# Attention and SwiGLU in one kernel: two-bank exps in the first batch, a ring of single PSUM banks, and x transposed by DMA from batch 2 on

## Chip, cores, metric

One core of one Trainium2 chip. The metric is the device time of one execution in microseconds; executions of one kernel here lie up to 1.4% apart (413.16 to 418.88 us for the kernel before). The profile is one such execution; its span is some 2 us shorter than the time.

## The reference

```python
# q, k, v: (8 batches, 8 heads, 576, 64), s: (8, 8, 576); x: (4608, 512)
cum    = np.cumsum(np.maximum(s, 0.0), axis=-1)
scores = q @ k.T / 8 + np.minimum(-(cum[..., :, None] - cum[..., None, :]), 0)   # causal
attn   = softmax(scores) @ v
x      = attn.transpose(0, 2, 1, 3).reshape(4608, 512)
out    = (silu(x @ w_gate) * (x @ w_val)) @ w_out                                # d_ff = 1536
```

## The kernel before

Per head, scores are computed transposed (keys on partitions), exponentiated, multiplied by V ("AV" below) and normalised into `ot`, tokens on partitions. The FFN needs x with features on partitions, so each pair of heads is transposed. Nine FFN tiles of 512 tokens are woven with the attention of the next batch: after every FFN step of four matmuls, `pump` emits the attention pieces that are due. The program fixes the order of emission for each engine and for the DMA queue of the sync engine (SP); in the traces of before, after, e3 and e4 no SP instruction that issues a DMA starts before the one ahead of it has ended. PSUM, the memory into which TensorE writes its results, is divided by these kernels into eight banks of 512 fp32 columns.

```python
# PSUM: three pools
scp = tile_pool("scp", bufs=3, PSUM); avp = tile_pool("avp", bufs=1, PSUM)
mp  = tile_pool("mp", bufs=4, PSUM)
...
def x_pe(pr):                                   # x of one pair of heads
    ...
    ps = mp.tile([128, S], BF16, tag="m", name="xps")
    for c in range(NCH):                        # 5 chunks of tokens: 4 x 128, 64
        n = 128 if c < 4 else TAIL
        nc.tensor.transpose(ps[:, c*128 : c*128+n], ot[0:n, c, :], ident[0:n, 0:n])
    n0 = TT - 64 * b
    nc.vector.tensor_copy(xts[b + 1][:, r, 0 : S - n0], ps[:, n0:S])
    nc.vector.tensor_copy(xts[b][:, r, TT - n0 : TT], ps[:, 0:n0])
...
# K/Q of head blocks 2 to 4 (a block is four heads), directly ahead of their scores
if not first and step == 0 and 2 <= h < NPE:
    ...
    cast_one(h, "k", nc.gpsimd); cast_one(h, "q", nc.gpsimd)
    ...
    for g in range(2):
        for nm in ("k", "q"):
            pe_transpose(h, nm, g)
            pe_out(h, nm, g, 0, nc.vector); pe_out(h, nm, g, 1, nc.scalar)
...
LAG = 1.65       # heads by which the FFN runs behind the attention
```

From block 5 on, K and Q are cast on GpSimd, stored to DRAM, and brought back by two large DMA transposes per block (`pk<-ks`, `pq<-qs`), on SP like all loads and stores except the weights.

The softmax here doesn't subtract the row's maximum and nothing guards it: scores larger than these inputs give would overflow.

## Time and profile before

| | before |
|---|---|
| time, median of the runs at the start | 414.88 us |
| span of the profiled run | 411.9 us |
| first FFN matmul | 36.3 us |
| one steady period (an FFN tile with eight heads) | 42.1 us |
| TensorE / VectorE / ScalarE / GpSimd busy | 93 / 61 / 51 / 30% |

Busy shares average over stages with different limits. I read periods from the first output copy (`ysb`) of one tile to that of the next. How SP waited in the kernel before is in its own list of waits (who waited for whom: us in total, times, longest); a queue that waits 141 us for results has that much room:

```profile
SPq L490 <- ACT ysb L489: 140.8, 28, 31.1
SPq L198 <- POOL cq L194: 40.8, 11, 4.5
SPq L198 <- POOL ck L194: 31.1, 6, 9.8
```

### The profile page before, as it was taken

How to read it: one execution, taken by the hardware profiler on the slowest of the kernel's cores; microseconds unless marked ns; L12 is line 12 of the kernel's file. 1: busy time of each engine (PE TensorE's matmuls, PEld its weight loads, DVE VectorE, ACT ScalarE, POOL GpSimd, SP SyncE). 2: the span in 40 equal slices, each digit the busy share in tenths (PEclk: the TensorE clock that was granted, in tenths of full speed). 3: DMA queues.
4: the chain of work that ended last, by engine and by line, in shares of the span. 5: the costliest groups of instructions: out<-in, count | busy, mean ns of one | idle time of the engine just before them, and what ended most of it. 6: DMA issues, size and time to landing. Idle time of an engine off the chain costs nothing.

```text
span 411.9 us, 7992 instructions
## 1 busy us (share of the span) xinstructions
PE 383.5 (93%) x3082; PEld 211.9 (51%) x3082; DVE 251.0 (61%) x494; ACT 212.0 (51%) x421; POOL 125.2 (30%) x224
## 2 busy tenths in 40 slices
PE   2687797989999999999999999999999999999996
PEld 1464454645555555555555555555555544444442
DVE  7846666366873588358844884479446733752750
ACT  7463665666555555456545564565556532322321
POOL 4783252743262316131623162316211110000000
PEclk9989998999999999999999999999999999999999
DMA  7999998466845793469346924681410002002002
GB/s 265 146 230 221 268 245 266 122 193 164 210 109 173 179 228 94 148 199 245 81 132 207 260 81 108 216 175 51 116 57 2 2 27 76 0 10 95 0 4 100
DMA packets 85335, 56.71 MB, mean 138 GB/s; under 512 B 65552, under 2 KB 69584, under 8 KB 85296
## 3 DMA queue, kind: packets, MB, share of 16 engines
q1 hardware_dynamic: 81360, 51.40, 44.8%
q0 software_dynamic: 3936, 4.79, 6.9%
q8 instruction: 24, 0.39, 0.4%
q14 instruction: 15, 0.12, 0.1%
HBM read 37.90 MB, written 15.93 MB: 131 GB/s over the span
## 4 chain that ended last, share of the span: by engine, by line
PE 90%; DVE 4%; DMA 2%; ACT 1%; POOL 1%; issue 1%; ACTq 0%; POOLq 0%
PE pg L457 23%; PE py L481 23%; PE pv L470 22%; PE sc L269 11%; PE av L305 7%; PE xps L337 3%; DVE kq L240 2%; DMA kq<-HL 1%; ACT pt L277 1%; DMA s_sb<-in_s_dram 1%; POOL vt L136 1%; PE tps L225 1%; DVE ot L321 1%; DVE c L167 0%; PE avm L305 0%
## 5 line engine op out<-in xcount | busy, mean ns | idle before, releaser
L277 ACT ACTIVATE pt<-sc 128x512 bf16<-128x512 f32 (+1 forms) x256 | 117.7, 505 | 56.2 <-PE sc L269 54.8
L464 DVE SCALAR_TENSOR_TENSOR pp<-th,pg 128x512 bf16<-128x512 bf16 x108 | 74.1, 686 | 63.8 <-ACT th L462 63.4
L457 PE MATMUL pg<-xt,wg 128*128 128x512 bf16 x432 | 111.8, 381 | 0.0
L470 PE MATMUL pv<-xt,wv 128*128 128x512 bf16 x432 | 110.9, 379 | 0.0
L462 ACT ACTIVATE th<-pg 128x512 bf16<-128x512 f32 x108 | 64.5, 597 | 86.0 <-PE pg L457 86.0
L481 PE MATMUL py<-wo,ht 128*128 128x512 bf16 x432 | 105.7, 379 | 0.0
L269 PE MATMUL sc<-kq 128*128 128x128 bf16 (+4 forms) x576 | 76.4, 247 | 10.4 <-DVE kq L240 5.5
L281 POOL TENSOR_SCALAR_AFFINE_SELECT pt<-pt 128x512 bf16<-128x512 bf16 x64 | 40.8, 637 | 140.0 <-ACT pt L277 137.7
L475 DVE TENSOR_TENSOR ht<-pp,pv 128x512 bf16<-128x512 bf16 x108 | 73.9, 684 | 7.9
L269 PEld LDWEIGHTS <-kq 128*128 128x128 bf16 x576 | 46.9, 101 | 44.3 <-issue 7.0
L457 PEld LDWEIGHTS <-wg 128*128 128x128 bf16 x432 | 38.5, 98 | 36.3 <-issue 0.8
L470 PEld LDWEIGHTS <-wv 128*128 128x128 bf16 x432 | 38.4, 98 | 34.8
L481 PEld LDWEIGHTS <-ht 128*128 128x128 bf16 x432 | 38.2, 98 | 34.9
L305 PEld LDWEIGHTS <-pt 128*128 128x128 bf16 x960 | 41.2, 98 | 20.9 <-issue 3.0
L305 PE MATMUL av<-vt,pt 128*128 128x65 bf16 x900 | 47.4, 194 | 2.0 <-POOL vt L136 0.9
L489 ACT ACTIVATE ysb<-py 128x512 f32<-128x512 f32 x36 | 21.5, 598 | 43.6 <-PE py L481 42.4
L286 POOL TENSOR_SCALAR_AFFINE_SELECT pt<-pt 128x64 bf16<-128x64 bf16 x64 | 15.4, 240 | 64.5 <-ACT pt L277 64.4
L341 DVE COPY xt<-xps 128x64 bf16<-128x64 bf16 (+7 forms) x32 | 9.7, 304 | 34.7 <-PE xps L337 34.7
L321 DVE TENSOR_TENSOR ot<-av,rc 128x320 bf16<-128x320 f32 x60 | 29.5, 491 | 2.1
L320 DVE RECIPROCAL rc<-av 128x5 f32<-128x5 f32 x60 | 11.4, 189 | 31.3 <-PE av L305 31.2
L136 POOL CAST vt<-rawv 128x512 bf16<-128x512 f32 (+1 forms) x40 | 25.7, 673 | 0.0
L240 DVE COPY kq<-tps 64x640 bf16<-64x640 bf16 (+1 forms) x24 | 17.5, 762 | 2.3 <-PE tps L225 2.1
(47 smaller groups left out, 160.6 us busy)
## 6 DMA issues: line engine op xcount, KB each, us to landing
rawk<-in_k_dram SPq DMA_DIRECT2D x16, 576.0 KB
rawq<-in_q_dram SPq DMA_DIRECT2D x16, 576.0 KB
out_dram<-ysb SPq DMA_DIRECT2D x36, 256.0 KB
rawv<-in_v_dram SPq DMA_DIRECT2D x32, 256.0 KB
ks<-ck SPq DMA_DIRECT2D x11, 288.0 KB
qs<-cq SPq DMA_DIRECT2D x11, 288.0 KB
wg<-in_moe_w_gate_dram POOLq DMA_DIRECT2D x2, 768.0 KB, 8.8
wv<-in_moe_w_val_dram POOLq DMA_DIRECT2D x2, 768.0 KB, 10.1
```

The lines of the kernel that those rows point to most:

```text
L136: eng.tensor_copy(VT[b % 2][0:n, c, :, 0:D], loaded["v", b][0:n, c, :, :])
L269: nc.tensor.matmul(sc[:, o : o + w], T[:, 0, e * S + 128 * tj : e * S + 128 * (tj + 1)], T[:, 1, e * S + lo : e * S + hi], start=True, sto ...
L277: nc.scalar.activation(pt[:, CHUNK_PT[ci] : CHUNK_PT[ci] + o], sc[:, 0:o], AF.Exp, scale=0.125)
L281: nc.gpsimd.affine_select(pt[:, 1088:1600], pt[:, 1088:1600], pattern=[[0, 4], [1, 128]], compare_op=ALU.is_ge, fill=zreg, base=0, channel ...
L305: nc.tensor.matmul(av[:, bi * (D + 1) : (bi + 1) * (D + 1)], pt[:, c0 : c0 + 128], VT[b % 2][:, tj, h, :], start=(tj == 0), stop=(tj == bi),)
L321: nc.vector.tensor_mul(ot[:, :, e * D : (e + 1) * D], av3[:, :, 0:D], rc[:, :, None].to_broadcast([128, NCH, D]),)
L457: nc.tensor.matmul(pg, WG[j][:, c, f0 : f0 + 128], xt[:, c, :], start=(c == 0), stop=(c == 3),)
L462: nc.scalar.activation(th, pg, AF.Tanh, scale=0.5)
L464: nc.vector.scalar_tensor_tensor(pp, in0=th, scalar=1.0, in1=pg, op0=ALU.add, op1=ALU.mult)
L470: nc.tensor.matmul(pv, WV[j][:, c, f0 : f0 + 128], xt[:, c, :], start=(c == 0), stop=(c == 3),)
L475: nc.vector.tensor_mul(ht, pp, pv)
L481: nc.tensor.matmul(py, hts[ft][:, ts_ * 128 : (ts_ + 1) * 128], WO[ft // WKO][:, ft % WKO, :], start=(ft == 0), stop=(ft == NFT - 1),)
```

## The change

The intent is to take x's transposes off TensorE, to halve the number of exps of batch 0, to let any PSUM bank serve any use, and to prepare K and Q of blocks 2 to 4 a block ahead. The core of the diff (cuts marked by ...):

```diff
-    scp = ... ; avp = ... ; mp = ...                       # three PSUM pools
+        bank["w", 0..1] = psa.tile([128, 1024], FP32)      # batch 0: two wide, four single
+        bank["s", 0..3] = psa.tile([128, 512], FP32)
+        ... second_psum(): eight single banks, taken in order of release
...
+            if b >= 2:                                     # in x_pe
+                for c in range(NCH):
+                    lo, end = c * 128, min(S, c * 128 + 128)
+                    while lo < end:
+                        hi = min(end, n0) if lo < n0 else end
+                        dst = (xts[b][:, r, TT - n0 + lo : TT - n0 + hi] if lo < n0
+                               else xts[b + 1][:, r, lo - n0 : hi - n0])
+                        nc.sync.dma_start_transpose(dst, ot[lo - c*128 : hi - c*128, c, :])
+                        lo = hi
+                return
...
+                if ahead and step == 0:                    # K/Q one block ahead
+                    cast_one(h + 1, "k", nc.gpsimd); cast_one(h + 1, "q", nc.gpsimd)
+                        if ahead and ci == 1 and step: prep_one(h + 1, step - 1)
...
-        load_v(0, range(5))
+        load_v(0, range(3))        # chunks 3, 4 later; w_load("g", 0), ("v", 0) earlier;
+                                   # casts of V at head 2 instead of head 1
-        LAG = 1.65
+        LAG = 2.65
```

More of the change, by code (lines that the diff above doesn't have):

```diff
@@ L51 @@
     NWCH = DF // WCH
-    DIAG_OFF = [1088, 1216, 1344, 1472, 1024]
-    OFF_OFF = {0: 0, 3: 448, 1: 512, 2: 832}
+    DIAG_OFF = [1088, 1216, 1344, 1472, 512]
+    OFF_OFF = {0: 576, 3: 1024, 1: 0, 2: 320}
     PTW = 1600
@@ L61 @@
     ]
-    CHUNK_PT = [1088, 0, 512, 1024]
+    CHUNK_PT = [1088, 576, 0, 512]
     def pt_col(tj, bi):
@@ L77 @@
     yp = ctx.enter_context(tc.tile_pool(name="yp", bufs=3))
-    scp = ctx.enter_context(tc.tile_pool(name="scp", bufs=3, space=PSUM))
-    avp = ctx.enter_context(tc.tile_pool(name="avp", bufs=1, space=PSUM))
-    mp = ctx.enter_context(tc.tile_pool(name="mp", bufs=4, space=PSUM))
     dram = ctx.enter_context(
@@ L105, with take, give, second_psum @@
         loaded = {}
-        SRC = {"k": (k, 0), "q": (q, 1)}
+        SRC = {"q": (q, 0), "k": (k, 1)}
+        first_psum = ExitStack()
+        psa = first_psum.enter_context(tc.tile_pool(name="psa", bufs=1, space=PSUM))
+        bank = {}
+        for i in range(2):
+            bank["w", i] = psa.tile([128, 1024], FP32, name=f"wide{i}")
+        for i in range(4):
+            bank["s", i] = psa.tile([128, 512], FP32, name=f"one{i}")
+        released = {key: i - 8 for i, key in enumerate(bank)}
+        clock = [0]
+        OPEN = 1 << 40
+        def take(kind="s"):
+            b = min((x for x in bank if x[0] == kind), key=lambda x: released[x])
+            assert released[b] < OPEN
+            released[b] = OPEN
+            return b
+        def give(b):
+            clock[0] += 1
+            released[b] = clock[0]
+        def second_psum():
+            assert all(x < OPEN for x in released.values())
+            at_end = dict(released)
+            first_psum.close()
+            psb = ctx.enter_context(tc.tile_pool(name="psb", bufs=1, space=PSUM))
+            bank.clear()
+            released.clear()
+            for i in range(8):
+                bank["s", i] = psb.tile([128, 512], FP32, name=f"bank{i}")
+                released["s", i] = at_end["w", i // 2] if i < 4 else at_end["s", i - 4]
+        def view(b, w):
+            return bank[b][:, 0:w]
+        def view16(b, w):
+            return bank[b][:, 0 : w // 2].bitcast(BF16)
         def load_one(hb, name, rs=(0, NR)):
@@ L136, in cast_v @@
             eng.tensor_copy(VT[b % 2][0:n, c, :, 0:D], loaded["v", b][0:n, c, :, :])
-        nc.sync.dma_start(s_sb, s.rearrange("b h n -> (b h) n"))
-        load_qk(0)
-        load_qk(1)
-        load_v(0, range(5))
         ONES2 = 1.0019378662109375
@@ L148, in aug_rows @@
             return KQ[i][r][r0 : r0 + 64, :, :].bitcast(FP32)
-        nc.vector.memset(warm, 0.0)
-        nc.scalar.activation(warm, warm, AF.Exp)
-        nc.vector.memset(one_s, 1.0)
-        nc.vector.memset(HL[:, 2:4, 0, :].bitcast(FP32), NEGS2)
-        nc.vector.memset(HL[:, 0:2, 1, :].bitcast(FP32), ONES2)
-        make_identity(nc, ident)
-        for e in range(2):
-            nc.gpsimd.memset(aug_rows(0, e)[:, 1, :], ONES2)
-            nc.gpsimd.memset(aug_rows(0, e)[:, 0, :], 0.0)
-            nc.scalar.copy(
-                KQ[1][e][64 * (1 - e) : 64 * (1 - e) + 64, 1, :],
-                one_s[:, 0:1].to_broadcast([64, NR * S + 64]),
-            )
-        nc.vector.memset(aug_rows(1, 0)[:, 0, :], 0.0)
-        nc.vector.tensor_scalar(s_sb, s_sb, 0.0, 8.0, ALU.max, ALU.mult)
-        nc.vector.tensor_tensor_scan(c8, one_s, s_sb, 0.0, ALU.mult, ALU.add)
-        nc.vector.tensor_copy(HL[:, 0, 0, :], c8)
-        nc.vector.tensor_sub(HL[:, 1, 0, :], c8, HL[:, 0, 0, :])
-        nc.vector.tensor_copy(HL[:, 2:4, 1, :], HL[:, 0:2, 0, :])
-        for r in range(2):
-            for i in range(2):
-                nc.vector.memset(KQ[i][r][64 * r : 64 * r + 64, :, NR * S :], 0.0)
         def aug(hb, engs):
@@ L178, in aug @@
                 r0 = 64 * (1 - r)
+                bh = hb * HB + hh
                 engs[hh].dma_start(
                     KQ[hb % 2][r][r0 : r0 + 4, :, e * S : (e + 1) * S],
-                    HL[hb * HB + hh : hb * HB + hh + 1, :, :, :],
+                    HL[bh : bh + 1, :, :, :],
                 )
+        nc.sync.dma_start(s_sb, s.rearrange("b h n -> (b h) n"))
+        load_qk(0)
+        load_qk(1)
+        load_v(0, range(3))
+        nc.vector.memset(warm, 0.0)
+        nc.scalar.activation(warm, warm, AF.Exp)
+        nc.vector.memset(one_s, 1.0)
+        nc.vector.memset(HL[:, 0:2, 0, :].bitcast(FP32), ONES2)
+        nc.vector.memset(HL[:, 2:4, 1, :].bitcast(FP32), NEGS2)
+        make_identity(nc, ident)
+        for r in range(2):
+            nc.gpsimd.memset(aug_rows(0, r), 0.0)
+            nc.scalar.mul(
+                KQ[1][r][64 * (1 - r) : 64 * (1 - r) + 64, 0, :],
+                one_s[:, 0:1].to_broadcast([64, NR * S + 64]), 0.0,
+            )
+        for r in range(2):
+            nc.gpsimd.memset(aug_rows(1, r)[:, 1, :], 0.0)
+            for i in range(2):
+                nc.gpsimd.memset(KQ[i][r][64 * r : 64 * r + 64, :, NR * S :], 0.0)
+        nc.vector.tensor_scalar(s_sb, s_sb, 0.0, 8.0, ALU.max, ALU.mult)
+        nc.vector.tensor_tensor_scan(c8, one_s, s_sb, 0.0, ALU.mult, ALU.add)
+        nc.vector.tensor_copy(HL[:, 0, 1, :], c8)
+        nc.vector.tensor_sub(HL[:, 1, 1, :], c8, HL[:, 0, 1, :])
+        nc.vector.tensor_copy(HL[:, 2:4, 0, :], HL[:, 0:2, 1, :])
         SP4 = [nc.sync] * 4
@@ L221, in pe_transpose @@
             j0, j1 = JG[g]
-            ps = mp.tile([128, j1 - j0, 128], BF16, tag="m", name="tps")
+            bs = take()
+            ps = view16(bs, (j1 - j0) * 128).rearrange("p (j x) -> p j x", x=128)
             ct = cts[name, hb]
@@ L227, in pe_transpose @@
                 )
-            tps[name, g] = ps
+            tps[name, g] = [ps, bs, 2]
         def pe_out(hb, name, g, r, eng):
@@ L235, in pe_out @@
             )[:, :, j0:j1]
-            srcp = tps[name, g][64 * r : 64 * r + 64].rearrange("a j x -> a x j")
+            tp = tps[name, g]
+            srcp = tp[0][64 * r : 64 * r + 64].rearrange("a j x -> a x j")
             if eng is nc.scalar:
@@ L240, in pe_out @@
                 eng.tensor_copy(dst, srcp)
+            tp[2] -= 1
+            if tp[2] == 0:
+                give(tp[1])
         def w_load(kind, j):
@@ L256 @@
         xts = {}
+        scs = {}
         def score_piece(bh, ci):
             hb, hh = divmod(bh, HB)
+            pair = bh < H
             if ci == 0:
@@ L264, in score_piece @@
             T = KQ[hb % 2][r]
-            sc = scp.tile([128, 512], FP32, tag="sc", name="sc")
-            o = 0
+            if pair:
+                if ci % 2 == 0:
+                    bs = take("w")
+                    scs[bh] = bs
+                else:
+                    bs = scs[bh]
+                base = (512, 0, 0, 512)[ci]
+            else:
+                bs = take()
+                base = 0
+            o = base
+            n = sum(hi - lo for _, lo, hi in CHUNKS[ci])
+            sc = view(bs, 1024 if pair else 512)
             for (tj, lo, hi) in CHUNKS[ci]:
@@ L270, in score_piece @@
                     sc[:, o : o + w],
-                    T[:, 0, e * S + 128 * tj : e * S + 128 * (tj + 1)],
-                    T[:, 1, e * S + lo : e * S + hi],
+                    T[:, 1, e * S + 128 * tj : e * S + 128 * (tj + 1)],
+                    T[:, 0, e * S + lo : e * S + hi],
                     start=True,
@@ L276, in score_piece @@
                 o += w
-            nc.scalar.activation(
-                pt[:, CHUNK_PT[ci] : CHUNK_PT[ci] + o], sc[:, 0:o], AF.Exp, scale=0.125
-            )
-            if ci == 0:
+            if not pair or ci % 2 == 1:
+                if pair:
+                    c0, W = ((576, 1024), (0, 576))[ci // 2]
+                else:
+                    c0, W = CHUNK_PT[ci], n
+                nc.scalar.activation(pt[:, c0 : c0 + W], sc[:, 0:W], AF.Exp, scale=0.125)
+                give(bs)
+            if ci == (1 if pair else 0):
                 nc.gpsimd.affine_select(
@@ L286, in score_piece @@
                 nc.gpsimd.affine_select(
-                    pt[:, 1024:1088], pt[:, 1024:1088], pattern=[[1, 64]],
+                    pt[:, 512:576], pt[:, 512:576], pattern=[[1, 64]],
                     compare_op=ALU.is_ge, fill=zreg, base=0, channel_multiplier=-1,
@@ L295, in av_piece @@
             if bis[0] == 0:
-                if b == 0 and h % 2 == 1:
-                    avs[bh] = mp.tile([128, NCH * (D + 1)], FP32, tag="m", name="avm")
-                else:
-                    avs[bh] = avp.tile([128, NCH * (D + 1)], FP32, tag="av", name="av")
-            av = avs[bh]
+                bs = take()
+                avs[bh] = (view(bs, NCH * (D + 1)), bs)
+            av = avs[bh][0]
             pt = pts[bh]
@@ L317, in av_out @@
             ot = ots[pr]
-            av3 = avs.pop(bh).rearrange("p (c e) -> p c e", e=D + 1)
+            av, bs = avs.pop(bh)
+            av3 = av.rearrange("p (c e) -> p c e", e=D + 1)
             rc = small.tile([128, NCH], FP32, tag="rc", name="rc")
@@ L325, in av_out @@
             )
+            give(bs)
             pts.pop(bh)
@@ L333, in x_pe @@
                     xts[tt] = xtp.tile([128, 4, TT], BF16, tag="xt", name="xt")
-            ps = mp.tile([128, S], BF16, tag="m", name="xps")
+            n0 = TT - 64 * b
+            if b >= 2:
[3 more added lines that the diff above has]
+                        hi = min(end, n0) if lo < n0 else end
+                        dst = (
+                            xts[b][:, r, TT - n0 + lo : TT - n0 + hi]
+                            if lo < n0
+                            else xts[b + 1][:, r, lo - n0 : hi - n0]
+                        )
+                        nc.sync.dma_start_transpose(
+                            dst, ot[lo - c * 128 : hi - c * 128, c, :]
+                        )
+                        lo = hi
+                return
+            bs = take()
+            ps = view16(bs, S)
             for c in range(NCH):
@@ L339, in x_pe @@
                 )
-            n0 = TT - 64 * b
             nc.vector.tensor_copy(xts[b + 1][:, r, 0 : S - n0], ps[:, n0:S])
             nc.vector.tensor_copy(xts[b][:, r, TT - n0 : TT], ps[:, 0:n0])
-        wlate = {
-            0: ("g", 0), 1: ("v", 0), 3: ("g", 1), 5: ("v", 1), 7: ("o", 0), 8: ("o", 1),
-        }
+            give(bs)
+        wlate = {2: ("g", 1), 4: ("v", 1), 8: ("o", 0), 9: ("o", 1)}
         def side(h, step):
@@ L352, in side @@
             if h == 0:
-                if step == 0:
-                    for g in range(2):
-                        for nm in ("k", "q"):
-                            pe_transpose(1, nm, g)
-                            pe_out(1, nm, g, 0, nc.vector)
-                            pe_out(1, nm, g, 1, nc.vector)
-                if step == 1:
+                if step == 1:
+                    for r in range(2):
+                        for g in range(2):
+                            for nm in ("k", "q"):
+                                if r == 0:
+                                    pe_transpose(1, nm, g)
+                                prep1.append((nm, g, r))
+                    for nm, g, r in prep1[:4]:
+                        pe_out(1, nm, g, r, nc.vector)
+                if step == 2:
                     for c in range(5):
                         cast_v(0, c, nc.gpsimd)
+                    for nm, g, r in prep1[4:6]:
+                        pe_out(1, nm, g, r, nc.vector)
+                if step == 3:
+                    for nm, g, r in prep1[6:8]:
+                        pe_out(1, nm, g, r, nc.vector)
                 return
@@ L367, in side @@
                     load_qk(2)
+                if step == 3:
+                    pass
                 return
@@ L403, in side, with prep_one @@
                         cast_v(bn, 4, nc.gpsimd)
+        prep1 = []
+        def prep_one(hb, i):
+            g, nm = divmod(i, 2)
+            nm = ("k", "q")[nm]
+            pe_transpose(hb, nm, g)
+            pe_out(hb, nm, g, 0, nc.vector)
+            pe_out(hb, nm, g, 1, nc.scalar)
         def attn_items():
@@ L411, in attn_items @@
                 h, step = divmod(bh, HB)
-                if not first and step == 0 and 2 <= h < NPE:
-                    if h > 3:
-                        aug(h, SP4)
-                    cast_one(h, "k", nc.gpsimd)
-                    cast_one(h, "q", nc.gpsimd)
-                    yield kk + 0.01
-                    yield kk + 0.02
-                    for g in range(2):
-                        for nm in ("k", "q"):
-                            pe_transpose(h, nm, g)
-                            pe_out(h, nm, g, 0, nc.vector)
-                            pe_out(h, nm, g, 1, nc.scalar)
-                            yield kk + 0.03 + 0.02 * g
+                ahead = not first and 2 <= h and h + 1 < NPE
+                if ahead and step == 0:
+                    if h + 1 > 3:
+                        aug(h + 1, SP4)
+                    cast_one(h + 1, "k", nc.gpsimd)
+                    cast_one(h + 1, "q", nc.gpsimd)
                 if first and bh == H:
@@ L435, in attn_items @@
                         yield kk + 0.1 + ci / 8
+                        if ahead and ci == 1 and step:
+                            prep_one(h + 1, step - 1)
+                            yield kk + 0.1 + ci / 8
+                        if ahead and ci == 3 and step == 3:
+                            prep_one(h + 1, 3)
+                            yield kk + 0.1 + ci / 8
                 x = bh - lag - 1
@@ L454, in ffn_items @@
                 j, f0 = divmod(ft * 128, WCH)
-                pg = mp.tile([128, TT], FP32, tag="m", name="pg")
+                gbs = take()
+                pg = view(gbs, TT)
                 for c in range(4):
@@ L466, in ffn_items @@
                 )
+                give(gbs)
                 yield 1
-                pv = mp.tile([128, TT], FP32, tag="m", name="pv")
+                vbs = take()
+                pv = view(vbs, TT)
                 for c in range(4):
@@ L475, in ffn_items @@
                 nc.vector.tensor_mul(ht, pp, pv)
+                give(vbs)
                 hts.append(ht)
@@ L478, in ffn_items @@
             for ts_ in range(4):
-                py = mp.tile([128, DM], FP32, tag="m", name="py")
+                ybs = take()
+                py = view(ybs, DM)
                 for ft in range(NFT):
@@ L489, in ffn_items @@
                 nc.scalar.mul(ysb, py, 0.5)
+                give(ybs)
                 nc.sync.dma_start(
@@ L499 @@
         cast_one(0, "k", nc.scalar)
-        nc.vector.memset(aug_rows(1, 1)[:, 0, :], 0.0)
         cast_one(0, "q", nc.vector)
         aug(0, [nc.gpsimd] * 4)
-        for nm, eng in (("k", nc.scalar), ("q", nc.vector)):
+        w_load("g", 0)
+        aug(1, SP4)
+        load_v(0, (3, 4))
+        for nm in ("k", "q"):
             for g in range(2):
                 pe_transpose(0, nm, g)
-                pe_out(0, nm, g, 0, eng)
-        for nm, eng in (("k", nc.scalar), ("q", nc.vector)):
-            for g in range(2):
-                pe_out(0, nm, g, 1, eng)
+        for r in range(2):
+            for nm, eng in (("k", nc.scalar), ("q", nc.vector)):
+                for g in range(2):
+                    pe_out(0, nm, g, r, eng)
         init_vt(0)
-        aug(1, [nc.gpsimd] * 4)
         cast_one(1, "k", nc.vector)
         cast_one(1, "q", nc.vector)
+        w_load("v", 0)
         at = attn_items()
@@ L523, in pump @@
                     state["pos"] = 1e9
-        LAG = 1.65
+        LAG = 2.65
         start = H + 2.45
         pump(start)
+        second_psum()
         hook = {
+            1: [lambda: cast_one(2, "k", nc.gpsimd), lambda: cast_one(2, "q", nc.vector)],
+            3: [lambda: prep_one(2, 0)],
+            4: [lambda: prep_one(2, 1)],
+            5: [lambda: prep_one(2, 2)],
+            6: [lambda: prep_one(2, 3)],
             21: [lambda: load_qk(5)],
@@ L534 @@
             span = 36
-            n0 = 6 if tt == 0 else 0
+            n0 = 7 if tt == 0 else 0
             n = 0
```

## The prediction

> **What bounds the kernel now.** I read the page first: busy shares, slices, chain of waits.
>
> ```profile
> PE 383.5 (93%) x3082; PEld 211.9 (51%) x3082; DVE 251.0 (61%) x494; ACT 212.0 (51%) x421; POOL 125.2 (30%) x224
> ...
> PE   2687797989999999999999999999999999999996
> ...
> PEclk9989998999999999999999999999999999999999
> ...
> PE 90%; DVE 4%; DMA 2%; ACT 1%; POOL 1%; issue 1%; ACTq 0%; POOLq 0%
> PE pg L457 23%; PE py L481 23%; PE pv L470 22%; PE sc L269 11%; PE av L305 7%; PE xps L337 3%; DVE kq L240 2%; DMA kq<-HL 1%; ACT pt L277 1%; DMA s_sb<-in_s_dram 1%; POOL vt L136 1%; PE tps L225 1%; DVE ot L321 1%; DVE c L167 0%; PE avm L305 0%
> ```
>
> The chain runs 90% through TensorE. TensorE is full from about slice 10 on; only the first nine slices (ten microseconds each) have holes, and in two of them the granted clock is lower too. So two things can shorten the kernel: less work for TensorE anywhere, and fewer holes in the first 90 us. More speed on ScalarE or VectorE after 90 us gains nothing.
>
> I then cut the busy time of the engines into stretches. Columns: start:end, length, then busy us and count of PE, PEld, DVE, ACT, POOL, granted clock, DMA share, GB/s.
>
> ```profile
> 43.00:48.10 5.10, 2.40 (x28) 1.72 (x27) 4.05 (x6) 2.83 (x5) 0.00 (x0) 1.00 1.08 234
> ...
> 62.00:70.00 8.00, 5.16 (x41) 2.99 (x40) 4.56 (x8) 4.24 (x8) 1.75 (x3) 0.79 1.01 328
> ...
> 84.00:88.30 4.30, 2.42 (x29) 1.80 (x28) 3.70 (x7) 2.89 (x5) 0.74 (x1) 1.00 0.43 121
> ...
> 134.60:176.70 42.10, 42.10 (x358) 23.49 (x357) 27.28 (x56) 23.40 (x50) 14.53 (x25) 1.00 0.64 167
> ```
>
> The first three rows are three holes: 2.70, 2.84 and 1.88 us without a matmul, 7.4 us in all. The last is one steady period (one 512-token FFN tile with eight heads woven in): no hole, VectorE at 65%, ScalarE at 56%, DMA at 64%. What causes the holes is in TensorE's timeline (start, length, instruction, idle time before it):
>
> ```profile
> 47.43 0.60 PE L269 MATMUL sc<-kq 128*128 128x128 bf16 x6 [2.30 <-DVE kq L240]
> ...
> 66.73 1.03 PE L269 MATMUL sc<-kq 128*128 128x128 bf16 x6 [2.30 <-DVE kq L240]
> ...
> 87.38 0.82 PE L269 MATMUL sc<-kq 128*128 128x128 bf16 x8 [0.87 <-DVE kq L240]
> ```
>
> At the start of head blocks 2, 3 and 4, K and Q are cast, transposed and copied in one piece directly ahead of the scores that need them, and TensorE waits for the copies. After the second hole the clock is lower: six score matmuls take 1.03 us where they took 0.60.
>
> **What the Trainium skill says.** (1) "VectorE: DVE Perf Modes", The three transpose paths: a 128×128 bf16 transpose takes 390 ns on TensorE, into PSUM, and 1309 ns through the DMA crossbar, into SBUF. This trace has single PE transposes at 219 ns, pipelined; no SBUF-to-SBUF DMA transpose runs in it. (2) "DMA: Bandwidth & Descriptors", DMA Transpose (X-bar), Constraints: only 2-byte types, issued by SP or ACT, destination SBUF. The diff obeys this, and issues them all on the SP queue, where the eleven pairs of K/Q transposes already run. (3) "ScalarE: Activation LUTs", What ACT_TABLE_LOAD costs: an ACTIVATE takes 186 ns + 0.833 ns per column, and two in a row overlap by about 93 ns. The trace agrees: 596 ns at 512 columns, 230 at 64; the four exps of a head in a row take 1.69 us, against 1600×0.833 + 4×93 = 1705 ns. (4) "TensorE: Matmul & The Clock Gate", What's actually happening: the clock halves after a window of some 3.4 us of idleness. The lower clock after the hole at 64 to 66.7 us fits.
>
> **The change part by part.**
>
> (a) *x transposes as DMAs from batch 2 on.* Each pair of heads has five PE transposes and two VectorE copies. The chain gives PE xps 2.9% of 411.9 us in its finer list: 11.9 us for 32 pairs, 0.373 us each. 24 of 32 pairs move: 24 × 0.373 = 9.0 us off TensorE, all in the stretch where it has no hole, so all of it counts. VectorE loses about 24 × 0.6 = 14 us, which is not on the path. Added are five or six SP transposes per pair (132 in all). Their cost: (i) data: around 161 to 166 us two existing transposes of 288 KB each are nearly alone on the DMA, and the DMA is busy 3.65 us of these five, so at most some 1.8 us for 288 KB; a batch of x is 590 KB, some 3.7 us per 42 us, which lifts the DMA share from 0.64 to about 0.73. (ii) SP issue: an existing transpose (nine times 128 rows) takes 1.2 to 1.3 us to issue, a plain copy 0.35 to 0.5. My estimate for 128 rows is 0.5 us; SP now issues some 26 us per period (read from its timeline, stalls included), so 22 more make 37 of 40.6 us: close, but below. (iii) latency: the last pair of a batch is issued at step 31 of the 36 FFN steps, because the lag of the FFN behind attention grows by one head. Five steps with the attention between them are about 6 us. Issue of three pieces (1.5 us) and about 2 us to land fit in it. Estimated waits: 0 to 3 us in total.
>
> (b) *K/Q of blocks 2 to 4 prepared ahead*, one quarter at a time between FFN or score pieces. The PE transposes stay, the waits go. Of the 7.4 us of holes I count 6.5 as gone, since with VectorE doing its 0.69 us FFN operations and 0.8 us copies in turn, the first block may still run VectorE-bound for a moment. The lower clock after the second hole goes too: pg 1.71 instead of 0.86, scores 1.03 instead of 0.6: 1.2 us.
>
> (c) *First batch with 1024- and 576-wide exps.* By the formula that the trace confirms, a head costs 1333 + 2×93 = 1.52 us of ScalarE in place of 1.70. The heads of batch 0 in fact come every 2.07 us (exps at 25.46, 27.53), since TensorE and ScalarE wait for one another in turn; with two wide buffers I work out about 1.8 to 1.85. That is 0.2 us for the last five heads or so, 1 to 1.3 us. Against it: the casts of V move behind head 2's select and one more weight-load issue on POOL. I put them at about 21.5 to 24.4 us where they ended at 22.5, and TensorE is stuck at head 0's AV until they are done: 1 to 1.8 us lost. Also the first exp starts only after six score matmuls instead of four. Net for the front: +0.5 us, uncertain by 2 either way. The first score still waits for the DMA of the cumulative sums at 13.6 us, which the change doesn't shorten.
>
> (d) *One ring of single PSUM banks for all uses.* Removes waits between score, AV and FFN buffers. TensorE has no such wait after 90 us, so 0.
>
> (e) *End of attention*: the last AV and x pieces now end inside tile 6; a hole of 0.9 us at 303 to 346 us goes: -0.9, and the DMA transposes of the last pair have 24 matmuls, 5 us, to land.
>
> Sum: -9.0 - 6.5 - 1.2 + 0.5 - 0.9 + 1.5 (DMA waits) = -15.6 us. A check from below: FFN starts at 36.8; nine tiles of 144 matmuls at 0.216 us are 279.9; 56 heads at 1.19 (from the steady period: (42.1 - 31.1 - 1.5)/8) are 66.6; three blocks of PE transposes 5; batch 1's x 1.5; the tail 4.0; together 393.8, plus 1 to 4 us of leftover waits. The two agree at 396 of span, that is 414.9 - 15.6 = 399 of time; I say 398.5.
>
> **The rivals.** R1: *SP becomes the bound.* If a 128-row transpose costs as much to issue as a 1152-row one (1.2 us), SP has 26 + 22×1.2 = 52 us per 40.6 us period; six periods would then grow by up to 11 us and the kernel would take 450 us or more. For it: only one size of transpose is in the trace. Against: the same 288 KB took 1.2 to 1.3 us of issue and nearly 2 us of DMA, so issue seems to go with rows. 4%. R2: *the transfer comes late.* FFN tiles 2 to 8 would start with TensorE waiting 1 to 3 us on DMA of xt, for instance because SP stands at an output store or behind large loads: +7 to 15 us, so the gain of (a) is eaten: 402 to 410. For it: DMA share is 0.64 already and SP waits in order. Against: the extra head of lag. 20%. R3: *the front gets worse by more than the 0.5* since V's cast is later and the first exp needs six matmuls; with +3 us the time is 401. R4: *the holes move rather than vanish*: head blocks 2 to 4 still wait for copies on a busy VectorE; half the gain of (b) kept: 402.
>
> **Range and chances.** The sure part is (a), 9 us of TensorE work, and most of (b). With the front ±2, (b) ±2 and DMA waits 0 to 8 us the 8-in-10 range is 391 to 409. The 2% line is 406.6; it falls only with R2 in its worse half or R1. Faster 0.87, same 0.11, slower 0.02.
>
> **What would show it right or wrong.** Right: xps on PE falls to 8 pairs (40 matmuls); the steady period shrinks from 42.1 to about 40.6 us with TensorE full; no wait of scores for kq copies over 0.5 us and a clock of 1.00 after the first FFN; FFN starts between 34.5 and 38.5 us. Wrong: pg waiting on a DMA of xt (R2), an SP timeline without gaps and transposes of over 1 us (R1), sc still waiting for DVE kq (R4), FFN starting after 39 us (R3).

## The result, and the profile after

The changed kernel takes 463.81 us (median of 4, 463.56 to 464.51), the kernel before 415.67 beside it. The ratio is 1.1156, 95% interval 1.1075 to 1.1237: 11.6% slower where 4% faster was predicted.

The page of the changed kernel, busy shares, slices and chain:

```profile
PE 388.6 (84%) x2962; PEld 209.8 (45%) x2962; DVE 237.0 (51%) x441; ACT 212.1 (46%) x405; POOL 122.9 (27%) x223
...
PE   1587899899994999369993999649996999999996
...
PEclk9978999999995999769997999779999899999999
...
PE 66%; SPq 14%; DMA 10%; DVE 4%; ACT 2%; issue 2%; POOL 1%; ACTq 0%; DVEq 0%; POOLq 0%
```

PEclk is TensorE's granted clock in tenths of full speed. The holes are now in the steady part, once per period, and the clock falls in and after them. The chain runs 14% through SPq, the issuing queue, which was not on it before. The pages' lines of the FFN's first matmul (gate), before and after, have the last column for idle time ahead of it:

```profile
L457 PE MATMUL pg<-xt,wg 128*128 128x512 bf16 x432 | 111.8, 381 | 0.0
L548 PE MATMUL bank<-xt,wg 128*128 128x512 bf16 x432 | 117.5, 394 | 37.3 <-DMA xt<-ot 36.5
```

The 36.5 us are five waits, one per tile from 2 to 6. TensorE's timeline has them; two of the rows, the first FFN matmul of a tile waiting for x:

```profile
144.97 0.58 PE L548 MATMUL bank<-xt,wg 128*128 128x512 bf16 x1 [7.14 <-DMA xt<-ot]
...
200.38 0.59 PE L548 MATMUL bank<-xt,wg 128*128 128x512 bf16 x1 [11.52 <-DMA xt<-ot]
```

A hole costs more than its length. In the record of the clock it drops to half about 2 us into each of these two holes and is full again only at 150.07 and 204.69 us, so 5.1 and 4.3 us of matmuls run at half speed. For the period of 55.0 us that closes the sum: 40.25 (a period without holes, see e4), 11.5 for this hole, 0.85 for a smaller one and an estimated 2.1 for the half clock make 54.7.

What SP did in the meantime is in its timeline (start, length, queue, line, what, count):

```profile
165.92 2.87 SPq L185 DMA_DIRECT2D kq<-HL  x4
168.88 7.98 SPq L402 DMA_TRANSPOSE xt<-ot  x6
177.31 0.36 SPq L232 DMA_DIRECT2D ks<-ck  x1
177.78 0.36 SPq L232 DMA_DIRECT2D qs<-cq  x1
179.60 1.23 SPq L242 DMA_TRANSPOSE pk<-ks  x1
180.93 1.24 SPq L242 DMA_TRANSPOSE pq<-qs  x1
182.26 8.05 SPq L402 DMA_TRANSPOSE xt<-ot  x6
190.35 0.58 SPq L147 DMA_DIRECT2D rawk<-in_k_dram  x1
190.98 0.47 SPq L147 DMA_DIRECT2D rawq<-in_q_dram  x1
191.55 2.84 SPq L185 DMA_DIRECT2D kq<-HL  x4
194.49 0.86 SPq L586 DMA_DIRECT2D out_dram<-ysb  x2
195.44 7.50 SPq L402 DMA_TRANSPOSE xt<-ot  x6
```

It is packed: but for two gaps of 0.4 and 1.5 us each instruction starts about 0.1 us or less after the end of the one before, and six transposes take 7.5 to 8.0 us. The last row is the last pair of the batch, of which this FFN tile uses the first three pieces; TensorE stands from 188.9 (200.38 - 11.52), 6.6 us before SP begins to issue them. The durations of the transposes by line (min/median/max in ns, of the changed kernel) and the stretches in which SP does nothing but issue them (DMA share and GB/s are the last two columns):

```profile
L402 SPq DMA_TRANSPOSE xt<-ot x132: 1092/1226/2366, 106.0 to 397.5; - x132
```

```profile
172.00:173.00 1.00, 1.00 (x14) 0.60 (x13) 0.25 (x1) 0.48 (x1) 0.14 (x1) 1.00 0.02 2
174.00:175.00 1.00, 1.00 (x7) 0.50 (x6) 1.00 (x2) 0.57 (x2) 0.47 (x1) 1.00 0.09 16
175.00:177.00 2.00, 2.00 (x22) 1.13 (x21) 0.06 (x1) 1.33 (x4) 0.41 (x2) 1.00 0.12 22
```

The DMA engines are 2 to 12% busy there. SP does not wait for data; it is issuing. What it does in the 1.2 us of one transpose is not in the trace. Its room has gone from the steady part: the durations of its issuing instructions, summed from the traces, are 18.1 to 20.0 us in each of four periods of 42.1 us before, and 46.7, 49.5, 46.7 and 50.4 us in the periods of 50.0, 55.0, 51.8 and 58.5 us after. In the first of these no gap between two of them is over 0.3 us. What is left of its waiting for output copies comes after the last transpose, which starts at 397.5 us:

```profile
SPq L586 <- ACT ysb L584: 55.7, 8, 22.8
```

The sum closes. From the first output copy of tile 1 to that of tile 6 the changed kernel takes 260.7 us (126.85 to 387.58) and the kernel before 210.5 (124.44 to 334.93): +50.2. Up to that first copy the changed kernel is 2.4 us later, after tile 6's it is 2.8 us shorter; together +49.8, against 461.8 - 411.9 = 49.9 of span.

### The profile page after: what moved, and what is told of

Read it like the earlier page. It is cut to its first block, busy times and chain, and to the rows that moved or that the text cites. A ratio compares the mean times of both kernels' runs of the same rounds, so it can differ in the third digit from the quotient of the medians.

```text
span 461.8 us, 7942 instructions
## 1 busy us (share of the span) xinstructions
PE 388.6 (84%) x2962; PEld 209.8 (45%) x2962; DVE 237.0 (51%) x441; ACT 212.1 (46%) x405; POOL 122.9 (27%) x223
## 4 chain that ended last, share of the span: by engine, by line
PE 66%; SPq 14%; DMA 10%; DVE 4%; ACT 2%; issue 2%; POOL 1%; ACTq 0%; DVEq 0%; POOLq 0%
PE bank L548 19%; PE bank L563 18%; PE bank L576 14%; SPq L402 7%; PE bank L322 7%; PE bank L360 4%; DMA xt<-ot 2%; SPq L185 2%; DMA rawv<-in_v_dram 2%; DMA pk<-ks 2%; DMA ks<-ck 2%; DMA rawk<-in_k_dram 2%; SPq L164 1%; SPq L242 1%; PE wide L322 1%
## 5 line engine op out<-in xcount | busy, mean ns | idle before, releaser
L548 PE MATMUL bank<-xt,wg 128*128 128x512 bf16 x432 | 117.5, 394 | 37.3 <-DMA xt<-ot 36.5
L555 DVE SCALAR_TENSOR_TENSOR pp<-th,bank 128x512 bf16<-128x512 bf16 x108 | 74.2, 687 | 130.1 <-ACT th L553 129.4
L335 ACT ACTIVATE pt<-bank 128x512 bf16<-128x512 f32 x224 | 104.4, 505 | 47.8 <-PE bank L322 42.3
L563 PE MATMUL bank<-xt,wv 128*128 128x512 bf16 x432 | 115.9, 392 | 1.9 <-DVE ht L568 1.9
L553 ACT ACTIVATE th<-bank 128x512 bf16<-128x512 f32 x108 | 64.6, 598 | 95.8 <-PE bank L548 93.6
L576 PE MATMUL bank<-wo,ht 128*128 128x512 bf16 x432 | 107.3, 385 | 0.0
L568 DVE TENSOR_TENSOR ht<-pp,bank 128x512 bf16<-128x512 bf16 x108 | 73.9, 685 | 10.4 <-PE bank L563 1.8
L322 PE MATMUL bank<-kq 128*128 128x128 bf16 (+4 forms) x504 | 68.9, 248 | 9.1 <-DVE ot L377 6.1
L322 PEld LDWEIGHTS <-kq 128*128 128x128 bf16 x576 | 48.8, 104 | 51.3 <-issue 18.8
L360 PE MATMUL bank<-vt,pt 128*128 128x65 bf16 x840 | 44.0, 195 | 2.3 <-POOL pt L343 1.8
L377 DVE TENSOR_TENSOR ot<-bank,rc 128x320 bf16<-128x320 f32 x56 | 27.5, 492 | 2.2 <-DVE rc L376 0.2
```

The lines of the kernel that those rows point to most:

```text
L322: nc.tensor.matmul(sc[:, o : o + w], T[:, 1, e * S + 128 * tj : e * S + 128 * (tj + 1)], T[:, 0, e * S + lo : e * S + hi], start=True, sto ...
L335: nc.scalar.activation(pt[:, c0 : c0 + W], sc[:, 0:W], AF.Exp, scale=0.125)
L360: nc.tensor.matmul(av[:, bi * (D + 1) : (bi + 1) * (D + 1)], pt[:, c0 : c0 + 128], VT[b % 2][:, tj, h, :], start=(tj == 0), stop=(tj == bi),)
L377: nc.vector.tensor_mul(ot[:, :, e * D : (e + 1) * D], av3[:, :, 0:D], rc[:, :, None].to_broadcast([128, NCH, D]),)
L548: nc.tensor.matmul(pg, WG[j][:, c, f0 : f0 + 128], xt[:, c, :], start=(c == 0), stop=(c == 3),)
L553: nc.scalar.activation(th, pg, AF.Tanh, scale=0.5)
```

## The experiments

Three theories. T1: each DMA transpose holds the in-order SP queue for about 1.23 us, whatever its size, so SP's issue time sets the period. T2: the transposed data land late, by their amount or the way through the DMA engines. T3: the PSUM ring or the early preparation does the harm. All kernels gave correct results; each was timed in three rounds against the kernel before, whose medians were 415.42 to 415.55 us.

**e1_x_on_pe.** Undo the x part alone.

```diff
-            if b >= 2:
+            if b >= B:
```

> The changed kernel with one part undone: all x transposes on TensorE again. T1 (each DMA transpose holds the in-order SP queue for 1.23 us, whatever its size) and T2 (the transposed data land late) both say that the four periods of 55 us fall back to 42, so 463.8 - 4 x 13 + about 4 (TensorE's extra work) = 415 +- 4 us. T3 (the PSUM ring or the early preparation is what hurts) says 440 or more. The front (FFN starts at 40.4 us instead of 36.3) should stay as in the changed kernel.

Measured: 414.30 us, ratio 0.9976 (0.9914 to 1.0038); periods of 42.1 us; FFN starts at 40.8. T3 falls: without the DMA transposes the rest of the change, in sum, makes no difference that the runs can tell.

**e2_before_plus_xdma.** The kernel before, plus the DMA transposes in `x_pe` and `LAG = 2.65`.

> The kernel before plus only the DMA transposes of x (and the lag 2.65 that gives them time). T1 and T2: about 46 us slower than before, 455 to 465 us, with periods near 55 us. T3: 405 to 418 us, as before or a little faster.

Measured: 466.17 us, ratio 1.1232 (1.1159 to 1.1305). This one part does all the harm (its edit holds two things, but e1 keeps the lag of 2.65 and does no harm).

**e3_merged_xdma.** The same data, neighbouring 128-column blocks of a pair in one instruction: 92 instead of 132. The core of the edit:

```diff
-    nc.sync.dma_start_transpose(dst, ot[lo - c*128 : hi - c*128, c, :])     # per block
+    nc.sync.dma_start_transpose(dst.rearrange("p (m x) -> p m x", x=128), ot[lo:hi, c:c1, :])
```

> The changed kernel, the same x data by DMA, but neighbouring 128-column blocks of a pair in one instruction: 92 transposes instead of 132 (3 per pair in even batches, 4 or 5 in odd ones). T1, issue time per instruction: 40 x 1.25 = 50 us less SP time, even periods PE-bound at 41 to 43 us, odd ones near 50: about 435 us. T2 (data): unchanged, 455 to 465 us. If issue time goes with the number of 128 blocks: unchanged too, with transposes of 2.4 to 3.7 us in the SP timeline.

Measured: 427.41 us, ratio 1.0280 (1.0216 to 1.0344), some 8 us better than T1's figure. In its SP timeline three transposes, one or two of them of several blocks, still take 3 x 1.25 us:

```profile
207.45 3.75 SPq L403 DMA_TRANSPOSE xt<-ot  x3
```

Periods alternate with the number of instructions: 40.3 and 40.9 us where a pair has three, 51.0 and 51.3 where it has five. SP issues for 37.0 and 37.4 us of the short ones, 44.7 and 44.9 of the long ones; the 6 us left there are gaps between issues. The data per period are the same in both. T2 falls, and so does the third possibility, an issue time that goes with the blocks.

**e6_aug_off_sp.** All 132 transposes stay on SP; only the small copies of the cumulative sums leave it.

```diff
-        SP4 = [nc.sync] * 4
+        SP4 = [nc.gpsimd] * 4
```

> The changed kernel, all 132 DMA transposes left on SP, but the small kq<-HL copies (8 per period, about 0.72 us of SP issue each) issued by GpSimd. T1: SP loses 5.8 us per period, so the long periods shrink from 55 to about 49 us and the time to 435 to 442 us. T2: unchanged, 460 us or more. GpSimd, busy 14 us of a period, has room for them.

Measured: 439.71 us, ratio 1.0571 (1.0517 to 1.0625), inside T1's range. Taking other issue work off SP helps although no transpose was touched.

**e4_two_per_pair.** x in one resident tile, so that no tile boundary cuts a pair: two transposes per pair, 48 in all.

```diff
+    XT = const.tile([128, 4, NT], BF16)             # ht 16 -> 13 buffers, y 3 -> 2
+    nc.sync.dma_start_transpose(
+        XT[:, r, t0 : t0 + 512].rearrange("p (m x) -> p m x", x=128), ot[:, 0:4, :])
+    nc.sync.dma_start_transpose(XT[:, r, t0 + 512 : t0 + S], ot[0:TAIL, 4, :])
```

> The changed kernel with x kept as one resident tile of all tokens, so that a pair needs two DMA transposes (four 128-column blocks in one, the 64-row tail in another): 48 instead of 132, the same data; to make room, 13 instead of 16 buffers for ht and 2 instead of 3 for y. T1: SP holds 26 + 8 x 1.25 = 36 us per period, below the 40.3 us that TensorE needs without x transposes, so all periods are TensorE-bound at 40.3: 414.3 (x on TensorE) - 5 x 1.8 = 405 +- 2 us, faster than the kernel before by about 2.5%. T2 (data): 455 to 465 us.

Measured: 402.57 us, ratio 0.9691 (0.9638 to 0.9743). SP issues for 29.6 to 31.5 us of a period. The two lines by duration (L390 moves four blocks, L394 sixty-four rows of one), and a period:

```profile
L390 SPq DMA_TRANSPOSE XT<-ot x24: 1209/1238/1985, 105.6 to 330.8; - x24
L394 SPq DMA_TRANSPOSE XT<-ot x24: 1209/1220/2405, 106.9 to 332.0; - x24
```

```profile
126.39:166.64 40.25, 39.88 (x335) 22.20 (x339) 25.15 (x48) 23.29 (x48) 14.28 (x26) 1.00 0.76 191
```

Eight times the elements, 18 ns more. With room on SP, TensorE is full again and its period is 1.85 us shorter than before; the DMA share of 0.76 harms nothing.

**f1_v_first, f2_weights_and_casts_as_before, f3_single_bank_exps.** The front, on the base of e1. FFN starts 4.1 us later in the changed kernel than before. Its ScalarE and GpSimd timelines in batch 0 (the time in brackets is idle time, and what ended it):

```profile
27.10 1.56 ACT L335 ACTIVATE pt<-wide 128x1024 bf16<-128x1024 f32 x2 [5.24 <-PE wide L322]
```

```profile
24.77 1.17 POOL L171 CAST vt<-rawv 128x512 bf16<-128x512 f32 x2 [0.32 <-DMA rawv<-in_v_dram]
```

The casts of V end at 25.9 us (22.5 before), TensorE stands at head 0's AV until then, and ScalarE starves for 5.24 us (2.15 before).

```diff
# f1                                  # f2: f1 and                          # f3
-load_v(0, range(3)); (3, 4) later    -w_load g0, v0 ahead of the heads     -pair = bh < H
+load_v(0, range(5))                  +weight loads at heads 0, 1, 3, 5, 7, 8  +pair = False
                                      +casts of V at head 1                 +eight single banks
```

> x on TensorE (e1), and the last two V chunks loaded ahead of the second block's small copies, as in the kernel before. If the late landing of V (24.8 us) holds the front up, FFN starts about 1 us earlier (39.8 instead of 40.8) and the time is 413.3; if it is the order on GpSimd (the casts begin at 22.7 us whatever has landed), 0.3 us or nothing.

Measured: 414.70 us, ratio 0.9985 (0.9938 to 1.0031), FFN starts at 39.85. No difference in time.

> x on TensorE (e1), V loaded first, the weight loads at their old places and the casts of V one head earlier, as in the kernel before. If the order on GpSimd ahead of head 0's AV is what costs the front, the casts end near 22.5 instead of 25.9 us and FFN starts at 37 to 38 us instead of 40.8: 411 +- 1.5 us. If not, 414.

Measured: FFN starts at 35.7 us, 5.1 earlier than in e1, but the time is 413.86 us, ratio 0.9974 (0.9927 to 1.0022). The front's delay is explained by the order of loads and casts, yet most of the gain is given back within tile 0: at its first output copy f2 is 0.8 us ahead of e1, at the end of the profiled run 1.7. In tile 0 TensorE waits 2.7 us in four pieces for V, from 55 to 58 us. GpSimd's timeline shows what stands ahead of V's casts, the cast of block 3 that the early preparation puts ahead of the casts of batch 1's V:

```profile
51.18 1.15 POOL L228 CAST ck<-rawk 128x1152 bf16<-128x1152 f32 x1 [16.95 <-DMA rawk<-in_k_dram]
```

> x on TensorE (e1), but batch 0 with 512-wide exps on a ring of eight single banks. If the two-bank exps gain what I predicted (1 to 1.3 us) FFN starts later by that, 42 us; if waiting for six matmuls and a ring of only two wide buffers costs more than it gains, FFN starts earlier, 39 to 40 us.

Measured: 411.26 us, ratio 0.9912 (0.9869 to 0.9955), FFN starts at 38.3. The two-bank exps, with the split of PSUM into wide and single banks that they need, cost 3.0 us by the medians of f3 and e1 and 4.0 us between the two profiled runs; g1 against e4 below gives 1.8 and 3.6. The intervals of the ratios of f3 and e1 overlap, so the sign is the same in both pairs but the size is uncertain. The first exp starts at 14.29 instead of 14.90 us, and batch 0's exps end at 35.2 instead of 37.1.

**p1_early_prep_alone.** The kernel before plus the early preparation of K and Q only (`prep_one`, its hooks, casts one block ahead).

> The kernel before plus only the early preparation of K and Q of blocks 2 to 4. My prediction's part (b) says 6.5 + 1.2 us less: 407.7. What e1 shows (FFN start to end only 3.0 us shorter than before, new holes where GpSimd waits for block 3's load) says 411 to 413 us.

Measured: 413.58 us, ratio 0.9943 (0.9890 to 0.9996), 1.9 us by the medians; the two profiled runs (before and p1) show no gain, 411.9 us of span each. The holes before the scores of blocks 2 and 4 (2.30 and 0.87 us) are gone, and 1.28 of 2.30 us is left at block 3. New are waits of 0.3 to 1.0 us each among FFN pieces from 42 to 47 us, where VectorE and ScalarE also copy K and Q, and 1.8 us at AV, which waits for V casts behind a GpSimd cast that waited 15.0 us for its load.

**b4_before_two_per_pair.** The kernel before plus e4's form of the x transposes only.

> The kernel before plus only the x DMA transposes in the two-per-pair form. T1: SP keeps below the period, TensorE loses 24 x 0.373 = 9.0 us: 406.4 +- 1.5 us, periods of 40.3 us in place of 42.1.

Measured: 405.94 us, ratio 0.9766 (0.9716 to 0.9816), as expected; periods of 40.2 to 40.3 us. The interval reaches over 0.98, so a gain of 2% is not settled by it, a gain is.

**g1_two_per_pair_single_banks.** e4 with f3.

> The changed kernel with two DMA transposes per pair (e4) and 512-wide exps in batch 0 on eight single banks (f3). If the two repairs add up: 402.6 - 3.0 = 399.6 +- 1.5 us.

Measured: 400.73 us, ratio 0.9645 (0.9591 to 0.9700), 1.1 us above the expected sum and within its range.

**g2_front_repaired.** g1 with f2, and block 3's casts behind those of V:

```diff
-                if ahead and step == 0: cast_one(h + 1, "k", ...); cast_one(h + 1, "q", ...)
                     side(h, step)                      # casts of V
+                    if ahead and step == 0: cast_one(h + 1, "k", ...); cast_one(h + 1, "q", ...)
```

> g1 with the weight loads, the V loads and the V casts of the first batch where the kernel before has them (f2), and GpSimd's casts of block 3 placed behind the casts of V instead of ahead of them. If the wait of GpSimd for block 3's load is what gave f2's earlier FFN start (35.7 us) back, this keeps 3 us or more of it: 395 to 398 us. If the DMA queue is what limits the first 65 us anyway, 399 to 400 us as g1.

Measured: 396.98 us (396.21 to 397.07), ratio 0.9540 (0.9498 to 0.9583): 4.6% faster than the kernel before, and the best kernel here. FFN starts at 33.6 us, and the cast no longer waits:

```profile
48.09 2.83 POOL L170 CAST vt<-rawv 128x512 bf16<-128x512 f32 x5
50.88 1.14 POOL L227 CAST ck<-rawk 128x1152 bf16<-128x1152 f32 x1
```

g2 has two edits over g1, so what each is worth alone is not shown. By the medians both together keep 3.7 us where f2 alone kept 0.4, which fits the GpSimd wait; between the profiled runs it is 2.3 against 1.7, so the evidence is weak. Nor is the wait simply gone: TensorE now stands 2.28 us at 52.1 us for this later cast, in place of f2's 2.7 us for V.

## Why the prediction was wrong

**The step that failed** is in part (a), (ii): "My estimate for 128 rows is 0.5 us", and under R1 "so issue seems to go with rows". Measured: 1.226 us for 128 rows, 1.220 for 64, 1.238 for four blocks, and for the old 1152-row ones medians of 1.25 to 1.61 (K and Q, before and after; the shortest 1.17). The time is per instruction: it does not grow from 64 rows to four blocks, and nine times the rows cost a third more at most. I had one size in the trace and read a slope into it, taking the rest from plain copies, another kind of instruction. The prediction's own alternative, R1, has the right mechanism and gives 52 us per period and 450 us or more; it was given 4%. Measured were 45 to 58 us and 464. That its 52 comes so near is in part luck: its 26 us for the rest of SP's work count stalls, where issue alone is 18 to 20 us before. With 20 the sum is 47 us, and SP's issue time measured 46.7 to 50.4; the rest of the longer periods are short gaps between the issues and a few waits for K or Q to be stored (the longest 2.92 us). The data that should decide were named ("only one size of transpose is in the trace"), but not weighed.

**Part (a), TensorE's saving**, was right: 9.0 us predicted, 9.5 from b4 (415.48 - 405.94), which has the saving without the SP bound (and the lag of 2.65 besides), and a period of 40.25 us where about 40.6 was predicted. **(i) the data**: a DMA share of about 0.73 was predicted, e4 has 0.76. **(iii) latency**: the extra head of lag was enough wherever SP had room (e4, b4).

**Part (b)** had the mechanism but not the size: 7.7 us predicted, 1.9 or less from p1. The old holes mostly go (in e1, with the whole change, 2.09 of 2.30 us stay at block 2), new ones come, since a block prepared ahead needs its load ahead as well, and GpSimd waits for it in order.

**Part (c)** had the wrong sign in its main term. Halving the number of exps was to gain 1 to 1.3 us; f3 and g1 show a cost of some 2 to 4. For the front in all +0.5 was predicted, +4.1 measured at the FFN's start, under R3's line of 39 us only in f2, f3 and the two kernels built from them, g1 and g2. R3 was right in naming the casts of V and the six matmuls ahead of the first exp.

**R2** (late transfer) and **R4** (holes that move) in their pure form: R2 is what TensorE's wait looks like ("DMA xt<-ot"), but e3 and e6 show that the transfer was late because it was issued late. R4 is what p1 shows, but it is small beside R1.

**The clock.** The prediction says that the lower clock after the hole at 64 to 66.7 us fits the skill's window of some 3.4 us of idleness. The trace does not show such a window: the clock dropped at 66.21 us, 1.8 us after the end of the last matmul, and the 3.4 us before that hold 1.08 us of matmul time.

Part (d), the ring of banks, and (e), the end of attention, were not run by themselves. e1 says only that all parts other than the x transposes are together worth between -0.9 and +0.4%.

## What to carry to other kernels

An in-order queue has a budget of issue time per period, as an engine has of busy time; add up all that a queue must issue, with the duration of the same kind of instruction, before moving work onto it. Where issue is per instruction, change the layout so that one instruction moves more: here one resident tile in place of three rotating ones took 132 transposes to 48, and 11.6% slower to 3.1% faster. When work is prepared earlier, look where its load stands in the queues, and what else waits behind it.

## What the Trainium skill lacked or had wrong

- "DMA: Bandwidth & Descriptors", DMA Transpose (X-bar), does not give the issue time of a transpose on this chip (elsewhere the page has cycles per instruction only in a table about trn3, in a column for earlier generations that it does not name). Here it is 1.22 to 1.24 us of SP per instruction (medians), the same for 64×128, 128×128 and four 128×128 blocks from SBUF, and 1.25 to 1.61 for 1152×128 from DRAM, while the DMA engines stand at 2 to 12%.
- "VectorE: DVE Perf Modes", The three transpose paths, gives 1309 ns for a 128×128 DMA transpose. The page doesn't say which time it means. The runs show two: 1.226 us in the issuing queue, where transposes don't overlap, and another 2.2 to 2.4 us on the chain from the end of issue to landing.
- No page of those that I read says that one transpose from SBUF may take several 128-column blocks at the cost of one; 24 four-block transposes took 1.238 us each (median).
